# Masked chunk scores in three 256-column banks instead of two 512-column ones

## The chip, the cores and the metric

The kernel runs on one core of a Trainium2 chip. The metric is device time in microseconds (us): the median of three runs before is 471.69 us (471.17 to 472.49). A profile is one further execution; its times are read against its own span and its own device time, both given below.

## The reference

Two blocks follow each other. The first is a gated recurrence over four batches, eight heads, 768 steps and a head width of 48; the second is a feed-forward block on the 3072 resulting rows of 384.

```python
for t in range(S):                                   # attention, per batch and head
    state = alpha[t, :, None] * state + outer(k[t], v[t])
    y[t] = q[t] @ state
a = x @ w1; b = x @ w2                               # x: y with the heads side by side
out = ((a * b) @ w3) @ w_out                         # 384 -> 1024 -> 1024 -> 384
```

## The kernel before

The sequence is cut into 24 chunks of 128 steps (six per batch). In a chunk the recurrence becomes small matrix products: with k and q scaled by the running decays, the scores k q are masked to the causal triangle and multiplied with v, and a carried state T adds what came from earlier chunks. Eight heads are worked as four pairs: index j is the pair, i the head in it, and head i sits on partitions 64i to 64i+47.

The main loop (L689) has one turn per chunk. In turn n TensorE gets, in this order: `attend_state(n-1)` (L469, state times q), `scores(n)`, `transposed(n+1)` (L376), `attend(n-1)` (masked scores times v, L477 or L480), `outer(n)` (L388), and at the end `decays(n+3)` (L341). Between them stand pieces of the first matrix products of the feed-forward block, which keep TensorE busy: a piece is nine products of `exact` (L510) on two PSUM banks. From turn 10 on the number of pieces repeats as 3, 3, 2, 0; turns 9, 13, 17 and 21 have none. After the loop (`part1.close()`, L785) the feed-forward block alone goes on, and nearly all of it is L510.

All PSUM results come from one pool of eight banks of 128 partitions by 512 fp32 (`bank()`, L105). The framework that builds the program gives each request the bank that is freed first in its own plan of the program, and makes the first product into it wait for the reader that frees it. So which reader a product waits for depends on how many banks were asked for before it. The readers that matter here are: the mask on VectorE (L435) for scores; two copies on ScalarE (L378) for transposes; two copies on ScalarE (L484) for the attention result y; an exponential on ScalarE (L345) for the decays; an add on VectorE (L398) for the outer product; a scaled copy on ScalarE (L519) and an add on VectorE (L521) for the two banks of a gate piece. Instruction order on every engine is fixed when the program is built; the same plan decides, within limits written in the code (`issue_after`), how independent work such as the weight conversion (L238 to L260) is woven in.

Scores of chunks 0 to 7 are whole 128x128 squares (`scores`, L441). From chunk 8 (`TURNED`, the ninth) on, `turned_scores` (L417) leaves out the quarter that the mask would empty. With 64x64 blocks A (first half of the steps against the first), B (second against second) and C (k of the first half against q of the second), a matmul of 128 columns gives A and C of a head, one of 64 columns gives B. For head i=1 the halves of the partitions are swapped ("turned"), so that blocks of both heads can run in different quarters of the array at once: array rows by i, array columns by `part ^ i`. `attend_low` (L414) multiplies the A blocks of the chunk before with v between the score products; `attend` (L477) does B and C together. The masked scores lie in the tile `ms`, and `keep` and `keep_turned` hold the masks as integers for a bitwise and.

Of the kernel before, what the change touches and what calls it, by code (L numbers as in the profile page):

```python
# [12 lines left out]
I32 = mybir.dt.int32  # L13
# [3 lines left out]
ALU = mybir.AluOpType  # L17
# [31 lines left out]
def kernel(  # L49
# [12 lines left out]
    nc = tc.nc  # L62
    B, H, S, D = q.shape
    C = 128
    DM = H * D
    DF = moe_w1.shape[1]
    NCH = S // C
    N = B * NCH
    NP = H // 2
    DP = 64  # L70
# [13 lines left out]
    def pool(name, bufs, stack=ctx, **kw):  # L84
        return stack.enter_context(tc.tile_pool(name=name, bufs=bufs, **kw))
# [15 lines left out]
    p1 = pool("p1", 1, stack=part1, side="right", reuse_waits="tile")  # L101
# [3 lines left out]
    def bank():  # L105
        return ps.tile([C, 512], FP32, tag="bank", name="bank")

    st, mark = {}, {}
# [51 lines left out]
    def turned(n):  # L160
        return TURNED <= n < N
# [28 lines left out]
    sums = p1.tile([C, 2, C], FP32R, name="sums")  # L190
    signs = p1.tile([C, 2, C], FP32R, name="signs")
    keep = p1.tile([C, C], I32, name="keep")
    keep_turned = p1.tile([C, 2, DP], I32, name="keep_turned")
    qks = [p1.tile([C, 2, H, DP], FP32, name=f"qk{i}") for i in range(3)]
    Ts = [p1.tile([C, NP, DP], FP32, name=f"T{i}") for i in range(2)]
    decs = [p1.tile([C, 3, NP], FP32, name=f"dec{i}") for i in range(2)]
# [8 lines left out]
    nc.vector.tensor_scalar_mul(keep, utri, -1.0)  # L205
    keep_bc = keep[:, None, :].to_broadcast([C, NP, C])
    for half in range(2):
        nc.gpsimd.tensor_copy(out=keep_turned[ds(DP * half, DP), 1 - half], in_=keep[ds(DP * half, DP), ds(DP * half, DP)])
    nc.gpsimd.memset(keep_turned[DP:, 1], -1)
    for x in qks:  # L210
        nc.vector.memset(x[:, :, :, D:], 0.0)
    make_identity(nc, ident)
# [197 lines left out]
    def attend_low(n, jj, i, half):  # L410

        s, w = ds(DP * i, DP), (vts[n % 2] if i else st["v", n])
        h = half * NP // 2 + jj
        nc.tensor.matmul(st["y", n][0][i][ds(DP * half, DP), jj, 0:DP], w[s, h if i else 2 * h, :],  # L414
                         st["ms", n][s, i, h, 0:DP], start=(n % NCH == 0 and jj == 0), stop=True, skip_group_check=True)

    def turned_scores(n):  # L417

        qkT = st["qkT", n]
        sc = [bank().rearrange("p (j c) -> p j c", j=NP) for _ in range(2)]  # L420
        for j in range(NP):
            for part in range(2):
                for i in range(2):
                    r, t = ds(DP * i, D), slice(DP * part, C)
                    nc.tensor.matmul(sc[i][ds(DP * (part ^ i), DP), j, t], qkT[r, 0, j, ds(DP * part, DP)],  # L425
                                     qkT[r, 1, j, t], start=True, stop=True)
            if turned(n - 1):
                for i in range(2):
                    attend_low(n - 1, j % 2, i, i ^ (j < 2))
        ms = work.tile([C, 2, NP, C], FP32, tag="ms", name="ms")  # L430
        for i in range(2):
            r = ds(DP * i, DP)
            low, high = (keep_turned[r, 0], keep_turned[:, 1]) if i else (keep[r, 0:DP], keep[:, DP:])
            for x, mask, t in ((slice(DP * i, DP * (i + 1)), low, slice(0, DP)), (slice(0, C), high, slice(DP, C))):
                masked = nc.vector.tensor_tensor(ms[x, i, :, t].bitcast(I32), sc[i][x, :, t].bitcast(I32),  # L435
                                                 mask[:, None, :].to_broadcast([x.stop - x.start, NP, DP]),
                                                 op=ALU.bitwise_and)
        ends_of_part1[0] = mark["ms", n] = masked.ins
        st["ms", n] = ms

    def scores(n):  # L441
        if turned(n):
            return turned_scores(n)
        qkT = st["qkT", n]
        sc = [bank().rearrange("p (j c) -> p j c", j=NP) for _ in range(2)]
        for j in range(NP):
            for i in range(2):
                r = ds(DP * i, D)
                nc.tensor.matmul(sc[i][:, j, :], qkT[r, 0, j, :], qkT[r, 1, j, :], start=True, stop=True)  # L449
        ms = work.tile([C, 2, NP, C], FP32, tag="ms", name="ms")  # L450
        for i in range(2):
            masked = nc.vector.tensor_tensor(ms[:, i].bitcast(I32), sc[i].bitcast(I32), keep_bc, op=ALU.bitwise_and)
        ends_of_part1[0] = mark["ms", n] = masked.ins
        st["ms", n] = ms
# [17 lines left out]
    def attend(n):  # L472
        (y, heads), ms, vc = st.pop(("y", n)), st.pop(("ms", n)), st.pop(("v", n))
        for j, i, to in heads:
            if turned(n):
                w = vts[n % 2][:, j, :] if i else vc[:, 2 * j, :]
                nc.tensor.matmul(to[:, DP:], w, ms[:, i, j, DP:], start=False,  # L477
                                 stop=(j % HP == HP - 1), skip_group_check=True)
            else:
                nc.tensor.matmul(to, vc[:, 2 * j + i, :], ms[:, i, j, :], start=(n % NCH == 0 and j % HP == 0),  # L480
                                 stop=(j % HP == HP - 1), skip_group_check=True)
        x = work.tile([C, HP, 2, C], FP32, tag="x", name="x", bufs=4)
        for i in range(2):
            copied = nc.scalar.copy(x[:, :, i], y[i])  # L484
        ends_of_part1[1] = copied.ins
        x = x.rearrange("p j i t -> p (j i) t")

        g, c = divmod(n, G)
        to = xd[g].rearrange("(b h d) t -> b d h t", b=2, d=D)
        for half in range(2):  # L490
            later.append((to[half, :, :, ds(c * C, C)], x[ds(DP * half, D)]))
# [197 lines left out]
    for n in range(N + 1):  # L689
# [16 lines left out]
        if n < N:  # L706
            scores(n)
        else:
            for j in range(NP):
                for i in range(2):  # L710
                    attend_low(n - 1, j % 2, i, i ^ (j < 2))
# [34 lines left out]
        if n:  # L746
            attend(n - 1)
# [52 lines left out]
    low, high = range(FH), range(FH, KF)  # L800
# [74 lines left out]
```

## Time and profile before

| | |
|---|---|
| median of three runs | 471.69 us |
| profiled execution, device time | 472.93 us |
| its span on the core | 471.2 us |
| granted TensorE clock | 0.996 |
| TensorE (PE) busy | 453.1 us, 96% |
| VectorE (DVE) busy | 363.5 us, 77% |
| ScalarE (ACT) busy | 278.9 us, 59% |
| 64 mask operations L435 | 6.9 + 6.8 + 6.5 + 6.5 us |
| first turned score product | 69.5 us after the span's start |
| last turned score product | 178.5 us |

In the profile, a line of the group list names the source line, engine, operation, tile written and tile read, shapes and count, then busy time and mean duration, then idle time of that engine just before it and what ended the wait. PEld is TensorE's weight load. One fp32 matmul of the program is two passes, thus two PE instructions (a transpose is one); fp32r products are one. PE durations include the flow through the array and overlap, so a stretch's length is read from starts, not from sums of durations.

### The profile page before, as it was taken

What the parts mean: (1) busy time and instruction counts of PE and PEld (TensorE: products, weight loads), DVE (VectorE), ACT (ScalarE), POOL (GpSimd) and SP (SyncE); (2) the same over time, 40 slices, a digit from 0 to 9 for tenths busy, and PEclk for the clock granted to TensorE, in tenths of its full rate; (3) what the DMA queues carried; (4) which work ended last, traced back from release to release, by engine and by line L of the source; (5) the groups of instructions that cost most, each with busy time, mean ns of one, the idle gap of its engine ahead of it and who ended that gap; (6) DMA issues with size and microseconds to landing.
All of it is one profiled execution on the core that took longest, in us unless ns stands there. A gap on an engine that the chain in (4) does not pass through costs nothing.

```text
span 471.2 us, 11168 instructions
## 1 busy us (share of the span) xinstructions
PE 453.1 (96%) x4360; PEld 430.4 (91%) x4360; DVE 363.5 (77%) x610; ACT 278.9 (59%) x552; POOL 96.0 (20%) x186
## 2 busy tenths in 40 slices
PE   4996999999999999999999999999999999999996
PEld 2675889898999989999999999999999999999996
DVE  2876997999979898999999968764542977766771
ACT  4864975767767554889787656554553633333330
POOL 6332243234313550222221111111011000000000
PEclk9999999999999999999999999999999999999999
DMA  9999999999999953566685433212013886555511
GB/s 182 251 189 247 239 226 207 222 218 207 203 207 209 266 141 116 170 185 220 205 297 190 133 124 101 85 50 85 35 51 111 245 243 184 176 160 167 173 52 50
DMA packets 145668, 80.36 MB, mean 171 GB/s; under 512 B 96240, under 2 KB 137456, under 8 KB 145616
## 3 DMA queue, kind: packets, MB, share of 16 engines
q1 hardware_dynamic: 139840, 64.44, 55.2%
q0 software_dynamic: 5776, 15.22, 10.3%
q8 instruction: 34, 0.56, 0.5%
q14 instruction: 18, 0.15, 0.1%
HBM read 57.58 MB, written 22.06 MB: 169 GB/s over the span
## 4 chain that ended last, share of the span: by engine, by line
PE 86%; DMA 5%; DVE 4%; ACT 3%; issue 1%; SPq 0%; DVEq 0%; ACTq 0%
PE bank L510 70%; DMA kq<-in_q_dram 3%; PE bank L425 3%; PE bank L376 2%; PE bank L477 2%; PE bank L469 2%; PE bank L612 1%; PE bank L388 1%; PE bank L338 1%; PE bank L341 1%; DMA raw<-in_moe_w_dram 1%; PE bank L480 1%; DVE qk L354 1%; PE bank L414 1%; PE bank L449 1%
## 5 line engine op out<-in xcount | busy, mean ns | idle before, releaser
L510 PE MATMUL bank<-x,w 128*128 128x384 f32 x1152 | 212.4, 338 | 1.9 <-DVE ms L435 0.9
L510 PEld LDWEIGHTS bank<-x,w 128*128 128x128 f32 x1152 | 199.9, 188 | 4.4 <-DVE ms L435 1.0
L510 PE MATMUL bank<-w3o,ab 128*128 128x384 f32 x576 | 100.2, 336 | 0.0
L510 PEld LDWEIGHTS bank<-w3o,ab 128*128 128x128 f32 x576 | 99.8, 188 | 0.0
L535 ACT ACTIVATE bank<-bank 128x384 f32<-128x384 f32 x96 | 45.6, 476 | 43.0 <-PE bank L510 42.8
L519 ACT ACTIVATE t<-bank 128x384 f32<-128x384 f32 x64 | 31.6, 495 | 54.8 <-PE bank L510 54.6
L585 POOL DMA_DIRECT2D abd<-ab x45 | 25.7, 570 | 143.4 <-DVE ab L571 126.8
L571 DVE TENSOR_TENSOR ab<-bank,r 128x384 f32<-128x384 f32 x44 | 24.4, 555 | 25.6 <-ACT bank L535 16.4
L378 ACT COPY qkT<-bank 128x512 f32<-128x512 f32 x48 | 26.0, 591 | 24.2 <-PE bank L376 24.2
L641 DVE TENSOR_TENSOR ab<-abl,ab 128x1024 fp32r<-128x1024 f32 x24 | 29.4, 1224 | 13.0 <-ACT ab L640 13.0
L640 ACT ACTIVATE ab<-abl 128x1024 fp32r<-128x1024 f32 x24 | 25.5, 1061 | 20.2 <-PE bank L510 18.0
L510 PE MATMUL bank<-wo,w3T 128*128 128x384 f32 x192 | 35.9, 334 | 0.0
L354 DVE TENSOR_TENSOR qk<-kq,e 128x768 f32<-128x768 f32 x24 | 23.3, 971 | 15.0 <-ACT e L345 7.5
L510 PEld LDWEIGHTS bank<-wo,w3T 128*128 128x128 f32 x192 | 33.5, 188 | 0.0
L243 ACT ACTIVATE power<-power,rebias 128x512 uint32<-128x512 uint32 (+1 forms) x36 | 25.1, 700 | 12.2 <-DVE power L242 12.1
L521 DVE SCALAR_TENSOR_TENSOR o<-bank,t 128x384 f32<-128x384 f32 x24 | 13.4, 557 | 22.4 <-issue 13.7
L642 DVE SCALAR_TENSOR_TENSOR ab<-ab,abl 128x1024 fp32r<-128x1024 f32 x24 | 29.2, 1219 | 0.0
L521 DVE SCALAR_TENSOR_TENSOR r<-bank,t 128x384 f32<-128x384 f32 x40 | 22.1, 552 | 6.8 <-ACT t L519 4.1
L245 DVE SCALAR_TENSOR_TENSOR mant<-mant,rest 128x512 f32<-128x512 uint32 (+1 forms) x36 | 23.6, 655 | 2.0 <-ACT rest L238 1.9
L238 ACT ACTIVATE rest<-raw 128x512 f32<-128x512 uint32 (+1 forms) x36 | 23.4, 652 | 1.0 <-DMA raw<-in_moe_w_dram 1.0
L166 POOL COPY vt<-v 64x192 f32<-64x192 f32 x32 | 19.4, 606 | 22.0 <-DMA v<-in_v_dram 21.0
L246 DVE SCALAR_TENSOR_TENSOR power<-raw,power 128x512 uint32<-128x512 uint32 (+1 forms) x36 | 23.3, 655 | 0.3 <-ACT power L243 0.2
(104 smaller groups left out, 685.9 us busy)
## 6 DMA issues: line engine op xcount, KB each, us to landing
raw<-in_moe_w_dram SPq DMA_DIRECT2D x28, 512.0 KB, 5.3
abl<-abd SPq DMA_DIRECT2D x24, 512.0 KB, 4.3
abd<-ab POOLq DMA_DIRECT2D x45, 192.0 KB, 3.1
xT<-xd POOLq DMA_DIRECT2D x9, 576.0 KB, 4.4
kq<-in_k_dram SPq DMA_DIRECT2D x24, 192.0 KB, 5.0
kq<-in_q_dram SPq DMA_DIRECT2D x24, 192.0 KB, 5.8
xd<-x SPq DMA_DIRECT2D x48, 96.0 KB, 3.9
out_dram<-o SPq DMA_DIRECT2D x24, 192.0 KB, 3.4
```

What stands on the lines that cost most here:

```text
L243: nc.scalar.activation(power, power, AF.Relu, scale=2.0 ** 23, bias=rebias)
L354: mark["qk", n] = nc.vector.tensor_mul(qks[n % 3][:, :, :, 0:D], st.pop(("kq", n)), st.pop(("e", n)).rearrange("p i (h d) -> p i h d", h=H ...
L378: mark["qkT", n] = nc.scalar.copy(qkT[:, :, :, ds(DP * half, DP)], tp[half]).ins
L510: nc.tensor.matmul(p, w[part][i], x[part][i], start=start and part == parts[0] and i == 0, stop=stop and part == parts[-1] and i == n - 1, ...
L519: nc.scalar.activation(t, p1, AF.Copy, scale=(1.0 + 1.0 / P) * scale)
L521: nc.vector.scalar_tensor_tensor(to, p2, scale, t, op0=ALU.mult, op1=ALU.add)
L535: nc.scalar.activation(p, p, AF.Copy, scale=1.0 + 1.0 / P)
L571: nc.vector.tensor_mul(ab, p, r[0])
L585: (nc.gpsimd if late else nc.sync).dma_start(out=abd[g][:, f, :], in_=ab)
L640: nc.scalar.activation(t[:, 0], ab, AF.Copy, scale=1.0 - 2.0 ** -13)
L641: nc.vector.tensor_sub(t[:, 1], ab, t[:, 0].bitcast(FP32))
L642: nc.vector.scalar_tensor_tensor(t[:, 2], t[:, 0].bitcast(FP32), -1.0 - 1.0 / P, ab, op0=ALU.mult, op1=ALU.add)
```

## The change

The three kinds of blocks A, B and C get a bank each in place of one bank per head. Bank 0 takes the A blocks of both heads (head 0 on the lower partitions, head 1 on the upper), bank 1 takes B and C of head 0, bank 2 takes B and C of head 1; each bank uses 256 of its 512 columns. The 128-column matmul becomes two of 64 columns, so a chunk has 24 score matmuls in place of 16. `keep_turned` has a third plane, so that each bank is masked over all 128 partitions by one operation: three operations of 128x256 in place of four on 64x256 or 128x256 parts with strided rows. `attend_low` and `attend` read the new places in `ms`; their products are the same. The tile `ms` has the same size, and its last quarter stays unused. At the start, GpSimd makes the masks with four copies and two memsets in place of two and one.

```diff
-    keep_turned = p1.tile([C, 2, DP], I32, name="keep_turned")
+    keep_turned = p1.tile([C, 3, DP], I32, name="keep_turned")
...
     for half in range(2):
-        nc.gpsimd.tensor_copy(out=keep_turned[ds(DP * half, DP), 1 - half], in_=keep[ds(DP * half, DP), ds(DP * half, DP)])
-    nc.gpsimd.memset(keep_turned[DP:, 1], -1)
+        for x in (0, 2 - half):
+            nc.gpsimd.tensor_copy(out=keep_turned[ds(DP * half, DP), x], in_=keep[ds(DP * half, DP), ds(DP * half, DP)])
+        nc.gpsimd.memset(keep_turned[ds(DP * half, DP), 1 + half], -1)
...
         nc.tensor.matmul(st["y", n][0][i][ds(DP * half, DP), jj, 0:DP], w[s, h if i else 2 * h, :],
-                         st["ms", n][s, i, h, 0:DP], start=(n % NCH == 0 and jj == 0), stop=True, skip_group_check=True)
+                         st["ms", n][s, 0, h, :], start=(n % NCH == 0 and jj == 0), stop=True, skip_group_check=True)
...
-        sc = [bank().rearrange("p (j c) -> p j c", j=NP) for _ in range(2)]
+        sc = [bank()[:, 0:NP * DP].rearrange("p (j c) -> p j c", j=NP) for _ in range(3)]
         for j in range(NP):
-            for part in range(2):
+            for x, part, t in ((0, 0, 0), (1, 1, 1), (1, 0, 1)):
                 for i in range(2):
-                    r, t = ds(DP * i, D), slice(DP * part, C)
-                    nc.tensor.matmul(sc[i][ds(DP * (part ^ i), DP), j, t], qkT[r, 0, j, ds(DP * part, DP)],
-                                     qkT[r, 1, j, t], start=True, stop=True)
+                    r = ds(DP * i, D)
+                    nc.tensor.matmul(sc[x + x * i][ds(DP * (part ^ i), DP), j, :], qkT[r, 0, j, ds(DP * part, DP)],
+                                     qkT[r, 1, j, ds(DP * t, DP)], start=True, stop=True)
...
         ms = work.tile([C, 2, NP, C], FP32, tag="ms", name="ms")
-        for i in range(2):
-            r = ds(DP * i, DP)
-            low, high = (keep_turned[r, 0], keep_turned[:, 1]) if i else (keep[r, 0:DP], keep[:, DP:])
-            for x, mask, t in ((slice(DP * i, DP * (i + 1)), low, slice(0, DP)), (slice(0, C), high, slice(DP, C))):
-                masked = nc.vector.tensor_tensor(ms[x, i, :, t].bitcast(I32), sc[i][x, :, t].bitcast(I32),
-                                                 mask[:, None, :].to_broadcast([x.stop - x.start, NP, DP]),
-                                                 op=ALU.bitwise_and)
+        ms = ms.rearrange("p i j c -> p (i j c)")[:, 0:3 * NP * DP].rearrange("p (x j c) -> p x j c", x=3, j=NP)
+        for x in range(3):
+            masked = nc.vector.tensor_tensor(ms[:, x].bitcast(I32), sc[x].bitcast(I32),
+                                             keep_turned[:, x:x + 1, :].to_broadcast([C, NP, DP]), op=ALU.bitwise_and)
...
-                nc.tensor.matmul(to[:, DP:], w, ms[:, i, j, DP:], start=False,
+                nc.tensor.matmul(to[:, DP:], w, ms[:, 1 + i, j, :], start=False,
```

## The prediction

> **What bounds the kernel now.** I read the page's shares and slices, then busy times by stage, the group list, the waits of the stretch with turned scores, and the timeline around the longest waits.
>
> ```profile
> PE 453.1 (96%) x4360; PEld 430.4 (91%) x4360; DVE 363.5 (77%) x610; ACT 278.9 (59%) x552; POOL 96.0 (20%) x186
> PE   4996999999999999999999999999999999999996
> DVE  2876997999979898999999968764542977766771
> ```
>
> TensorE is full from the fourth slice on. VectorE is nearly as full until slice 23. By stage:
>
> ```profile
> 69.00:190.00 121.00, 118.86 (x2076) 109.88 (x2076) 108.79 (x212) 77.29 (x175) 38.13 (x69) 1.00 0.88 199
> 190.00:471.00 281.00, 277.54 (x1620) 276.93 (x1618) 203.60 (x310) 154.19 (x280) 32.21 (x53) 1.00 0.46 145
> ```
>
> After 190 us TensorE runs 277.5 of 281 us on work that the change does not touch: whatever part 1 loses or gains on TensorE moves the end by as much. From 69 to 190 VectorE is 90% busy (third figure), but only what makes TensorE wait counts. Its waits there:
>
> ```profile
> PE bank L510 <- DVE ms L435: 0.9, 2, 0.7
> PE bank L510 <- ACT qkT L378: 0.5, 1, 0.5
> PE bank L469 <- DVE ms L435: 0.3, 1, 0.3
> PE bank L425 <- ACT w L255: 0.2, 1, 0.2
> ```
>
> These are understated, since a matmul's modelled end covers the start of a gap. From the starts of single products, less the usual spacing, I get seven stalls, 2.85 us: 0.65 at 87.1 (bank freed by a copy L378), and 0.31 at 96.3, 0.37 at 110.9, 0.41 at 111.8, 0.14 at 140.1, 0.08 at 152.6, 0.89 at 173.8, whose bank a mask L435 frees: 2.2 us by masks. (The 0.2 put down to L255 is the 0.41 at 111.8: in the program that product waits for the fourth mask.)
>
> **What the Trainium skill says.** "TensorEngine Tiling (Array Packing)", Key Properties: tiles of the array work independently, and a change of tiling mode drains it. The trace agrees: score starts in each quarter keep their own rhythm, and 146 ns pass from the last 64-column start to the transposes, in place of about 60. "TensorE: Matmul & The Clock Gate", Part 3, says matmuls start strictly in program order; here they don't:
>
> ```profile
> 78.40 0.38 PE L425 MATMUL bank<-qkT 48*64 48x128 f32 x7
> 78.52 0.22 PE L414 MATMUL bank<-ms,v 64*64 64x64 f32 x1
> ...
> 78.53 0.27 PE L425 MATMUL bank<-qkT 48*64 48x128 f32 x1
> ```
>
> Eight score passes stand ahead of the first L414 in the program, and seven had started. The trace decides. "VectorE: DVE Perf Modes", Two Vector instructions with no wait between them: an operation whose operand starts in another group of 32 partitions than the last one's is held until earlier ones finish. The trace fits: mask 2 starts 0.33 us after mask 1 (both start at partition 0), mask 3 (partition 64) 0.44 after 2, mask 4 (0 again) 0.44 after 3. "PSUM — Partial Sum Buffer", Specifications, gives eight banks; the kernel's pool has all.
>
> **The change, part by part.**
>
> ```profile
> L425 PE MATMUL bank<-qkT 48*64 48x128 f32 x256 | 18.8, 271 | 0.2 <-ACT w L255 0.2
> L425 PE MATMUL bank<-qkT 48*64 48x64 f32 x256 | 16.0, 226 | 0.0
> L435 DVE TENSOR_TENSOR ms<-bank,keep_turned 64x256 int32<-64x256 int32 x16 | 6.9, 428 | 0.5
> L435 DVE TENSOR_TENSOR ms<-bank,keep_turned 128x256 int32<-128x256 int32 x16 | 6.8, 425 | 0.2
> L435 DVE TENSOR_TENSOR ms<-bank,keep 64x256 int32<-64x256 int32 x16 | 6.5, 407 | 0.0
> L435 DVE TENSOR_TENSOR ms<-bank,keep 128x256 int32<-128x256 int32 x16 | 6.5, 405 | 0.0
> ```
>
> *Score products.* In a quarter, 128-column passes start every 109 ns and 64-column ones every 58 (a run of nine in 524 ns). The two loaded quarters had 8 x 109 = 872 ns a chunk and get 16 x 58 = 928; the other two keep their 8 passes and run beside them. So the block grows by 0.05 us, to 1.27 from the measured 1.22. 16 x 0.052 = +0.83 us, all on the path. Bounds: half of 109 gives -0.2; 62 (what the transposes take) gives +2.0.
>
> *Masks.* Start to next start: 0.33 + 0.44 + 0.44 + 0.34 = 1.55 us a chunk. All three new ones start at partition 0, so should not be held: 3 x 0.33 = 1.0; held, 1.3. VectorE saves 16 x 0.55 = 8.8 us (at least 4). This is worth only what it takes off the 2.2 us.
>
> *Mask set-up* on GpSimd: three more operations of 0.15 to 0.23 us before 5 us; `sums`, which the first decay product needs, comes no later in the order built, so nothing. Memory traffic is the same.
>
> *The ninth bank request.* A turn without gate pieces asks for y 2, scores 2, transposes 2, outer 1, decays 1: eight, one round of the pool. With three score banks it is nine on eight, so each request reaches one release further. In the order built, on turns 10, 14, 18 and 22 the outer product (L388) or transposes wait for a reader that ran later, and so do the gate pieces behind:
>
> ```profile
> 84.74 0.62 PE L388 MATMUL bank<-v,qk 128*64 128x48 f32 x16
> 85.29 1.32 PE L510 MATMUL bank<-x,w 128*128 128x384 f32 x6
> 87.11 1.15 PE L510 MATMUL bank<-x,w 128*128 128x384 f32 x5 [0.49 <-ACT qkT L378]
> ```
> ```profile
> 84.70 0.52 ACT L345 ACTIVATE e<-bank 128x384 f32<-128x384 f32 x1
> 85.86 0.72 ACT L243 ACTIVATE power<-power,rebias 128x512 uint32<-128x512 uint32 x1 [0.64 <-DVE power L242]
> 86.49 1.05 ACT L378 COPY qkT<-bank 128x512 f32<-128x512 f32 x2
> ```
>
> Turn 10: today the outer product waits for an L484 long done, the first six gate products use the bank that L345 freed at 85.23, and the seventh waits for L378's first copy (87.07). Afterwards L388 waits for L345, and the *first* gate product for that L378. The six products that covered the wait now come after it: 6 x 0.19 = +1.16. ScalarE's copy is itself late because it stands behind L243.
>
> Turn 14: the stalls of 0.37 and 0.41 go, VectorE having saved six chunks; but TensorE then reaches L388 0.8 earlier and meets L345 (ends 113.82, was 0.4 ahead): 0.45 back, and 0.3 for a gate bank that the first mask frees: 0. Turn 18: -0.14; L345 ends 142.68, L388 would start at 142.37: +0.44; the tenth gate product waits for the first mask (145.2), +0.3: +0.6. At 151.4 a gate's first bank is now the first mask's (ready 152.12, and 0.14 to react): 0.9, less 0.3 for an earlier VectorE, less the 0.08: +0.5. Turn 22: -0.89; transposes wait for L484 (+0.4) and the tenth gate product for a mask (+0.7): +0.2. At 96.3 the stall goes: -0.31. Sum of waits: 1.16 + 0 + 0.6 + 0.5 + 0.2 - 0.3 = +2.15. What queues behind each wait on TensorE is all later work.
>
> *Order before chunk 8.* The new plan also reorders turns 5 and 6: ScalarE puts L243 ahead of both L484 copies, and L255 ahead of L319; VectorE puts L257 ahead of both L452 masks of chunk 6. L484 (50.55 and 52.43) ends at 53.05, so the transposes start 0.26 later; L319 moves behind a 0.6 us operation, which delays the decay product 0.16 more; and L271, in need of the bank that the first L452 frees, goes from 55.41 to 56.28 (L257 ends near 55.45, the mask 0.7 later). +0.87, with no gap on TensorE behind it until 85 to give it back.
>
> Sum: 0.83 + 2.15 + 0.87 = **+3.85 us**. The profiled execution's span becomes 475.1 (its own device time, 472.93, lies 1.7 above its span); on the median of 471.69 this gives **475.5 us**.
>
> **Rivals.**
>
> *VectorE relief pays.* All 2.2 us of mask stalls vanish and no longer reach is felt: 0.83 - 2.2 = -1.4, 470.3 us, so faster. For it: VectorE is 90% busy and frees six of seven stalled banks. It decides if L345 ends 0.6 us before L388 asks, on turn 10 (85.22 against 84.74) and after; the trace shows it 0.5 too late. With the early reordering it is 471.2, no change. Together 6%.
>
> *TensorE's own cost alone*: banks wait as long as before, +0.83, 472.5 us. It needs slack in the pool, and the turns without pieces have none. 10%.
>
> *The quarters don't run ahead.* If the three pairs of products per j go in lockstep, a j takes 3 x 2 x 58 = 348 ns where the loaded quarters need 232: 4 x 116 = 0.46 a chunk, 7.4 in all, 482.9 us. The timeline at 78.5 speaks against it. 5%.
>
> That the change doesn't do what it says is out: the built program has three masks and 24 products a chunk.
>
> **How the numbers follow.** Forecast 79%, rivals 6, 10 and 5. Low end: 58 becomes 54.5 (-0.2), all mask stalls go, ScalarE's stay (1.16 + 0.45 + 0.44 + 0.4 - 2.2 = 0.25), early +0.87: +0.9, 472.6. High end: 62 ns and held masks (+0.6): +5.7, 477.4. About 0.3% (1.4 us) is what a measurement here tells from no change; from the cases: slower 0.86, same 0.10, faster 0.04.
>
> **What would show it.** Score blocks 0.05 us longer and three masks 0.33 apart; L271 near 56.3; L388 on turn 10 waiting for L345 and then no gate product before L378's copy ends. Wrong if VectorE's saving shows as fewer stalls with none on ScalarE, if score blocks pass 1.4 us, or if TensorE's time after 190 us changes.

## The result, and the profile after

| | median | runs | ratio to before, 95% interval |
|---|---|---|---|
| before | 472.49 us (471.17 to 472.72) | 5 | |
| after | 475.69 us (474.61 to 476.46) | 5 | 1.0074 (1.0053 to 1.0095) |

The change costs 3.2 us. Ratios here and below compare mean times and leave out executions more than 1.5% above the fastest of the same kernel (five of the two masks with smaller stores, one of the kernel before). The profiled execution took 475.83 us with a span of 474.0 us; the one before had 472.93 and 471.2, so the two traces differ by 2.8 us. The shares and slices of the page after:

```profile
PE 456.3 (96%) x4616; PEld 432.8 (91%) x4616; DVE 356.6 (75%) x594; ACT 279.4 (59%) x552; POOL 95.6 (20%) x189
PE   4998999899999999999999999999999999999996
DVE  1896896989869687999999968855542877666761
```

VectorE lost 7 us of work (363.5 to 356.6) and TensorE gained 3. By stage (span of the stretch, then busy time and instructions of PE, PEld, DVE, ACT and POOL, then clock, DMA share and GB/s):

```profile
69.00:192.00 123.00, 118.88 (x2327) 110.47 (x2327) 101.21 (x193) 76.74 (x174) 36.66 (x69) 1.00 0.89 198
192.00:474.00 282.00, 278.36 (x1625) 277.77 (x1623) 204.32 (x312) 155.05 (x282) 32.55 (x53) 1.00 0.46 146
```

I matched the starts of TensorE's products in the two traces, in order. Where a distance after minus before is given below, it is from that. It is -0.14 us at 67 us, +2.82 at 184 us and unchanged from there to the end. So all of the loss comes from the stretch with turned scores. TensorE's waits there, as the list of waits has them (engine, line, releaser: total us, times, longest):

```profile
PE bank L508 <- DVE ms L434: 1.8, 4, 0.8
PE bank L508 <- ACT qkT L379: 1.0, 1, 1.0
PE bank L426 <- issue: 0.7, 1, 0.7
PE bank L415 <- POOL vt L166: 0.4, 1, 0.4
PE bank L389 <- ACT e L346: 0.2, 1, 0.2
```

(After the change L426 is the score product, L434 the mask, L377 the transpose, L379 its copy, L389 the outer product, L415 a product of the A blocks with v, L508 a gate product, L342 the decays, L346 their exponential.) Waits for a mask are 1.8 us in four places, where the same list before had 1.2 in three, although VectorE has less to do. Four things are new: gate products wait for the copy of the transposes at their start, score products stop for nothing that the trace names, products of A wait for a copy on GpSimd, and the outer product of turn 14 waits for the exponential, as the prediction had it there.

*The products and masks.* The groups by shape, and the three masks of chunk 9 on VectorE's timeline:

```profile
L426 PE MATMUL bank<-qkT 48*64 48x64 f32 x768 | 20.3, 221 | 0.7 <-issue 0.7
L434 DVE TENSOR_TENSOR ms<-bank,keep_turned 128x256 int32<-128x256 int32 x48 | 17.4, 413 | 0.3 <-PE bank L426 0.3
```
```profile
79.68 1.08 DVE L434 TENSOR_TENSOR ms<-bank,keep_turned 128x256 int32<-128x256 int32 x3
```

Three masks take 1.08 us; with 0.41 for the last one they start 0.33 apart. The block of score products of chunk 9 goes from its first product to the first transpose. Before it began at 78.40, as the prediction shows; this is its end on TensorE's timeline of before, then both lines of after:

```profile
79.61 0.40 PE L376 MATMUL bank<-ident,qk 64*128 64x64 f32 x6
```
```profile
78.31 0.33 PE L426 MATMUL bank<-qkT 48*64 48x64 f32 x9
...
79.59 0.40 PE L377 MATMUL bank<-ident,qk 64*128 64x64 f32 x6
```

1.28 us in place of 1.22. Wherever nothing else stops the block, it is 0.054 to 0.057 longer: 0.9 us for 16.

*Turn 10.* TensorE's timeline after, then ScalarE's:

```profile
83.69 0.21 PE L426 MATMUL bank<-qkT 48*64 48x64 f32 x1 [0.73 <-issue]
...
85.75 0.62 PE L389 MATMUL bank<-v,qk 128*64 128x48 f32 x16
87.38 3.39 PE L508 MATMUL bank<-x,w 128*128 128x384 f32 x18 [1.01 <-ACT qkT L379]
90.61 0.51 PE L342 MATMUL bank<-la,sums 128*128 128x384 f32 x2
```
```profile
86.14 0.72 ACT L244 ACTIVATE power<-power,rebias 128x512 uint32<-128x512 uint32 x1 [0.97 <-DVE power L243]
86.76 1.05 ACT L379 COPY qkT<-bank 128x512 f32<-128x512 f32 x2
```

Before, six gate products ran from 85.29 and the seventh at 87.11, once its bank was copied. Now none runs until the first copy of the two is out (half of 1.05 us after 86.76), and all 18 come behind it. The decays L342 begin at 90.61, against 89.32 before.

### The profile page after: what moved, and what is told of

The parts are those of the page before. It is cut to its first block, busy times and chain, and to the rows that moved or that the text cites. A ratio compares the mean times of both kernels' runs of the same rounds, so it can differ in the third digit from the quotient of the medians.

```text
span 474.0 us, 11644 instructions
## 1 busy us (share of the span) xinstructions
PE 456.3 (96%) x4616; PEld 432.8 (91%) x4616; DVE 356.6 (75%) x594; ACT 279.4 (59%) x552; POOL 95.6 (20%) x189
## 4 chain that ended last, share of the span: by engine, by line
PE 83%; DVE 8%; ACT 3%; issue 3%; DMA 2%; SPq 0%; DVEq 0%; ACTq 0%
PE bank L508 70%; PE bank L426 2%; PE bank L377 2%; PE bank L467 2%; PE bank L610 1%; DMA kq<-in_q_dram 1%; DVE x L502 1%; PE bank L475 1%; PE bank L336 1%; DVE qk L355 1%; ACT x L500 1%; DVE ms L450 1%; ACT qkT L379 1%; PE bank L342 1%; PE bank L389 1%
## 5 line engine op out<-in xcount | busy, mean ns | idle before, releaser
L508 PE MATMUL bank<-x,w 128*128 128x384 f32 x1152 | 211.8, 338 | 3.0 <-DVE ms L434 1.8
L508 PEld LDWEIGHTS bank<-x,w 128*128 128x128 f32 x1152 | 200.0, 188 | 5.0 <-DVE ms L434 2.7
L508 PE MATMUL bank<-w3o,ab 128*128 128x384 f32 x576 | 100.2, 336 | 0.0
L508 PEld LDWEIGHTS bank<-w3o,ab 128*128 128x128 f32 x576 | 99.9, 188 | 0.0
L379 ACT COPY qkT<-bank 128x512 f32<-128x512 f32 x48 | 26.1, 596 | 26.4 <-PE bank L377 26.4
L508 PE MATMUL bank<-wo,w3T 128*128 128x384 f32 x192 | 35.9, 334 | 0.0
L508 PEld LDWEIGHTS bank<-wo,w3T 128*128 128x128 f32 x192 | 33.5, 188 | 0.0
L501 DVE TENSOR_TENSOR x<-xT,x 128x1152 fp32r<-128x1152 f32 x14 | 19.0, 1356 | 4.8 <-ACT x L500 4.7
```

The source lines that it names most:

```text
L379: mark["qkT", n] = nc.scalar.copy(qkT[:, :, :, ds(DP * half, DP)], tp[half]).ins
L508: nc.tensor.matmul(p, w[part][i], x[part][i], start=start and part == parts[0] and i == 0, stop=stop and part == parts[-1] and i == n - 1, ...
```

## The experiments

Each experiment was timed beside the kernel before on the same chip. In the four groups of experiments the kernel before had medians of 472.41 us (27 executions: early order, cut products, two masks, third bank), 472.63 (43: eight requests, four masks, and the kernel before and the cut products with smaller stores), 472.55 (28: the whole change, the two masks and the bare request with smaller stores) and 472.60 (27: third bank with smaller stores).

**The mask set-up and the early order alone.** The kernel before with the third plane of `keep_turned`, made by the four copies and two memsets of the change; the masks read the same values from other places. The build of it moves the same early instructions as the change does.

```diff
-    keep_turned = p1.tile([C, 2, DP], I32, name="keep_turned")
+    keep_turned = p1.tile([C, 3, DP], I32, name="keep_turned")
...
-            low, high = (keep_turned[r, 0], keep_turned[:, 1]) if i else ...
+            low, high = (keep_turned[r, 0], keep_turned[:, 2]) if i else ...
```

> The kernel before with nothing but the mask set-up of the change: three planes, made by four copies and two memsets; scores and the four masks as before. In the order built it carries the same swap on turns 5 and 6 as the change (L243 ahead of both L484, L255 ahead of L319, L257 ahead of both L452). Forecast's theory: the swap costs 0.87 us on TensorE, so +0.9 us (ratio 1.002), L271 0.9 us later against its neighbours. Rival: the part before chunk 8 is paced by loads and by VectorE, which give it back before 57 us: 0 us, and TensorE reaches the first gate product (about 58.3 us) no later than before.

Measured: 472.49 us (22 executions), ratio 1.0005 (0.9988 to 1.0021). No cost of the early order shows. The interval reaches to +1.0 us and so doesn't exclude 0.87 by itself; the traces do. TensorE is 0.6 us ahead of the kernel before at 67 us here, and the product of the weight conversion that the prediction put at 56.28, with VectorE's L257 ahead of it, came no more than 0.2 us late (the kernel before, this one, the kernel after):

```profile
55.41 0.69 PE L271 MATMUL bank<-w,signs 128*128 128x512 f32 x1
...
55.33 0.69 PE L272 MATMUL bank<-w,signs 128*128 128x512 f32 x1
...
55.60 0.50 PE L272 MATMUL bank<-w,signs 128*128 128x512 f32 x1
```

**Products cut in two, nothing else.** Two banks and four masks as before, 24 products of 64 columns.

```diff
-            for part in range(2):
+            for part, half in ((0, 0), (1, 1), (0, 1)):
...
-                    r, t = ds(DP * i, D), slice(DP * part, C)
+                    r, t = ds(DP * i, D), ds(DP * half, DP)
```

> The kernel before with only the products cut: each 128-column score product becomes two of 64 columns into the same two banks; four masks as before. 24 products a chunk. Theory: each score block 0.055 us longer, 16 blocks, +0.9 us (ratio 1.002), no wait moved to another reader. Rival, TensorE's own cost is the bulk of the change's +3.2 us, by more instructions to fetch and issue: +2.5 us or more, with gaps inside score blocks that no semaphore ends.

Measured: 476.82 us (6 executions), ratio 1.0086 (1.0063 to 1.0109). The blocks are 0.057 us longer, as expected, but that is 0.9 us of 4.4: in size the rival's value came, though the gap isn't in a score block. TensorE stops for 3.3 us in the middle of an outer product whose instructions wait for no semaphore, and from 115.8 us on the granted clock is 0.50 for 6.8 us (second fence: a stretch as above, which ends just after that; its mean clock, 0.54, stands after the five engines):

```profile
113.01 0.27 PE L388 MATMUL bank<-v,qk 128*64 128x48 f32 x2
116.37 0.99 PE L388 MATMUL bank<-v,qk 128*64 128x48 f32 x14 [3.10 <-issue]
```
```profile
118.00:123.00 5.00, 5.00 (x18) 5.00 (x18) 1.25 (x2) 0.98 (x2) 1.99 (x4) 0.54 0.83 152
```

The packets of the trace point to what stops it: a transfer of 16 KB on the instruction queue runs from 113.97 to 114.90, and TensorE goes on 1.48 us after its end. Every stop of this kind ends so. In the 14 traces of this case there are 14 stops of 0.35 us or more (from one start of a weight load to the next) between 60 and 192 us that no semaphore explains and that fall inside a run of like instructions; all end 1.28 to 1.61 us after such a transfer. In the kernel after, the transfer ended at 82.19 and the score products went on at 83.69. The six kernels with 24 products a chunk have ten of the stops, 13.1 us together, or 2.2 each; the other eight have four, 2.8 us together. In the whole execution the queue has 36 transfers in the kernel after and 34 in the kernel before:

```profile
q8 instruction: 36, 0.59, 0.6%
```
```profile
q8 instruction: 34, 0.56, 0.5%
```

That the transfers carry TensorE's instructions is worked out, not shown: 34 of 16 KB are 64 bytes for each of its 8,720 products and weight loads, and 36 the same for 9,232. And that the stops wait for the transfers rests on this agreement in time; no run changed these transfers alone.

**Two masks, two banks.** Full 128-column products throughout; the quarter that the mask empties is computed, too, and each bank is masked by one 128x512 operation, for which `keep_turned` becomes a whole 128x128 mask.

```diff
-                    r, t = ds(DP * i, D), slice(DP * part, C)
+                    r, t = ds(DP * i, D), slice(0, C)
...
+            mask = keep_turned if i else keep
+            masked = nc.vector.tensor_tensor(ms[:, i].bitcast(I32), sc[i].bitcast(I32),
+                                             mask[:, None, :].to_broadcast([C, NP, C]), op=ALU.bitwise_and)
```

> Two banks per chunk as before, but the 64-column product is widened to 128 columns too (the quarter that the mask empties is computed and masked away), so that each bank is masked by one operation of 128x512: two masks, no third bank, 16 products. Theory: the score block stays at 1.22 us, because the quarters that get more were idle; two masks take 2 x 0.60 = 1.2 us in place of 1.55, free the banks after 0.68 and 1.28 us in place of 0.79 and 1.68, and with no ninth request no wait moves to ScalarE: about half of the 2.2 us of mask stalls goes, -1 us (ratio 0.998). Rival, VectorE's time is worth nothing here: 0 us. Rival, the quarters are not independent: block 1.5 us or more, +4 us.

Measured: 477.92 us (6 executions), ratio 1.0117 (1.0097 to 1.0138). None of the three expected values came. The block stays at 1.22 us with a third more score columns in it, so the quarters of the array do run independently, and the two that had spare time fill it. The time goes in one place. TensorE's and GpSimd's waits between 107 and 118 us:

```profile
PE bank L413 <- POOL vt L166: 3.9, 1, 3.9
POOL dec L404 <- DMA dec<-ends: 5.1, 1, 5.1
```

GpSimd waits for a small transfer of its own and does the copy that TensorE needs only after that; the clock is 0.50 for 6.8 us from 113.2 us on, while TensorE still waits. So this run doesn't tell what VectorE's time is worth.

**A third bank request alone.** The kernel before with one more bank per chunk, an 8-column product into it and a small copy out of it (result unused).

```diff
+        extra = bank()[0:DP, 0:8]
+        nc.tensor.matmul(extra, qkT[0:D, 0, 0, 0:DP], qkT[0:D, 1, 0, 0:8], start=True, stop=True)
...
+        nc.vector.tensor_copy(out=work.tile([DP, 8], FP32, tag="extra", name="extra"), in_=extra)
```

> The kernel before with a third bank asked for in each turned chunk: one extra product of 8 columns into it (its result is not used) and one VectorE copy of 64x8 ahead of the masks, which frees it. Two score banks, 16 + 1 products, four masks. Theory, the ninth request is what costs: waits as in the change without VectorE's relief, so +2.5 to +3.5 us (ratio 1.005 to 1.007), on turn 10 no gate product before the copy L378 ends, 1.2 us later than before. Rival, the request is harmless and only the work counts: 16 x 0.1 us on TensorE's path at most, +0.3 to +1.0 us, and the first gate product on turn 10 starts when the outer product ends.

Measured: 476.32 us (6 executions), ratio 1.0073 (1.0046 to 1.01). Turn 10, TensorE's timeline:

```profile
87.28 0.67 PE L388 MATMUL bank<-v,qk 128*64 128x48 f32 x16 [0.24 <-ACT e L345]
89.14 4.09 PE L513 MATMUL bank<-x,w 128*128 128x384 f32 x13 [1.19 <-ACT qkT L378]
```

This is what the prediction foresaw for the change: the outer product waits for L345, and the first gate product waits for the copy L378. The request with its small product does it, with 16 score products and four masks as before. The time, at the top of the expected range, is not clean: in this trace the clock is halved for 3.4 us after this wait and for 6.8 us at 52 us, and the extra product costs 0.087 us per block, 1.4 us for 16.

**Eight requests again.** The kernel after, with the outer product written into free columns of the first score bank of its chunk.

```diff
-        s1 = bank()[:, 0:NP * D].rearrange("p (j d) -> p j d", j=NP)
+        s1 = (st.pop(("free", n)) if turned(n) else bank())[:, 0:NP * D].rearrange("p (j d) -> p j d", j=NP)
...
-        sc = [bank()[:, 0:NP * DP].rearrange("p (j c) -> p j c", j=NP) for _ in range(3)]
+        banks = [bank() for _ in range(3)]
+        st["free", n] = banks[0][:, NP * DP:]
+        sc = [x[:, 0:NP * DP].rearrange("p (j c) -> p j c", j=NP) for x in banks]
```

> The changed kernel (24 products of 64 columns and three masks a chunk), but the outer product L389 writes into columns 256 to 447 of the first score bank of its own chunk instead of asking for a bank, so that a turn without gate pieces asks for eight banks again. Theory (the ninth request costs what the moved waits cost, about 2.1 us): the first gate product of turn 10 no longer waits 1.0 us for the copy that frees its bank, and the time comes to 0 to +0.9 us over the kernel before, 472.4 to 473.4, which is 2 us or more below the changed kernel's 475.7. Rival 1 (the cost lies in the products and whatever they do to other work, not in the banks): it stays at 475 to 477. Rival 2 (transfers set the pace up to 120 us, and whoever runs ahead of them stalls for 4 us and runs on a halved clock, as the two kernels with a split product or two masks did near 113 us): 476 to 478, with a stall of over 3 us between 105 and 120 us.

Measured: 479.01 us (6 executions), ratio 1.013 (1.0106 to 1.0154): none of the three. The edit brought a wait of its own, because the outer product now has to wait for the mask that reads its bank, of the same chunk. Its line in the list of waits between 60 and 192 us, and turn 10 on the timeline:

```profile
PE bank L389 <- DVE ms L436: 4.3, 6, 1.3
```
```profile
85.81 1.32 PE L510 MATMUL bank<-x,w 128*128 128x384 f32 x6
87.30 0.61 PE L510 MATMUL bank<-x,w 128*128 128x384 f32 x2 [0.18 <-ACT qkT L379]
```

As a price of the request it failed. For turn 10 it is telling all the same: with eight requests, three masks and 24 products, six gate products run ahead of the copy again, as in the kernel before.

**VectorE's saving taken back.** The kernel after with its first mask as two operations of 64 partitions.

> The changed kernel with its first mask cut into two operations of half the partitions, so that VectorE does four operations a chunk again and each bank comes free 0.1 to 0.4 us later. If VectorE's saving is worth something in the changed kernel (the waits for a mask, 1.8 us in all, grow with it), 0.5 to 2 us above the changed kernel: 476.2 to 477.7. If it is worth nothing, 475.2 to 476.2.

Measured: 477.53 us (6 executions), ratio 1.01 (1.0078 to 1.0123), so 1.2 to 1.8 us above the kernel after, as expected if the saving counts. It does not follow that the saving is worth that: waits for a mask at the gate products are 1.8 us here as there, and the trace is 2.1 us longer from 62 us on with two stops without a semaphore (1.8 us at 82 us, 1.3 at 116) where the kernel after had one of 1.0, and a half-clock window at 84 us. The worth of the saving stays open in the changed kernel.

**The same with fewer bytes to move.** The stops at 110 to 118 us come behind a stretch in which the DMA engines are busy all the time: in the cut products their share is 1.04 from 108 to 113 us. (In the stop itself, from 114 to 116, it falls to 0.13, so the engines weren't full to its end.) So I cut the stores of the first two groups' gate results from 384 columns to 8. Their issues and waits stay; the rest of these results isn't stored, and the last stage reads the third group's in their place, so these kernels serve for timing only. I ran the kernel before and its parts with that.

```diff
+            w = 8 if g < 2 and not late else TG
-            (nc.gpsimd if late else nc.sync).dma_start(out=abd[g][:, f, :], in_=ab)
+            (nc.gpsimd if late else nc.sync).dma_start(out=abd[g][:, f, 0:w], in_=ab[:, 0:w])
...
-            nc.sync.dma_start(out=st["abl", n], in_=abd[g][:, :, ds(c * C, C)])
+            nc.sync.dma_start(out=st["abl", n], in_=abd[max(g, 2)][:, :, ds(c * C, C)])
```

> The kernel before, with the stores of the first two groups' gate results cut from 384 columns to 8 (the rest of these results is not stored, and the last stage reads the third group's in their place): about 190 KB less per store, some 20 stores between 75 and 140 us, all issues and waits kept. It is the measure for the next kernel. If the kernel before is seldom held by transfers: 470.5 to 472.5. If transfers set its pace: below 470.

> The kernel with nothing but the products cut in two (measured at 476.8, with a stall of 3.3 us at 113 us and a halved clock after it), with the same smaller stores as the kernel before in this call (the rest of the first two groups' gate results is not stored). If the stall is transfers that come late in a stretch where all queues are full, it goes, and the kernel is 0.9 us above the lightened kernel before (at most 1.5). If the stall belongs to the products themselves (more instructions to be fetched, or the order of the work), it stays, and the kernel is 3 to 5 us above it.

> The changed kernel with the smaller stores of the lightened kernels (of the first two groups' gate results only 8 of 384 columns are stored, and the last stage reads the third group's in their place). The lightened kernel before came to 472.1. Theory (products +0.9, ninth request about +2.1, neither having to do with transfers): 3 us above that, 474.6 to 475.8. If the changed kernel's loss comes from transfers that land late: 1.5 us or less above it, up to 473.6.

> The kernel before with a third score bank asked for and used by one 8-column product and one 64x8 copy (result unused), with the smaller stores of the lightened kernels. The extra product lengthens each of the 16 score blocks by 0.087 us, as measured with full stores: 1.4 us. Theory (the ninth request itself costs about 2.1 us, transfers or not): 3.5 us above the lightened kernel before (472.1), 474.9 to 476.2. If the request costs nothing and the kernel with full stores lost the rest by late transfers and a halved clock: 473.2 to 473.8.

> The kernel with two whole-bank masks, two score banks and 128-column products throughout (it computes the empty quarter and masks it), with the same smaller stores. With full stores it took 477.9, 5.5 us more than the kernel before, and stalled 3.9 us at 110 us on a tile of v that had not come, with a halved clock after it. If that is transfers: the stall goes, VectorE's saving takes up to 2.2 us of mask waits, and it is at or below the lightened kernel before, 470 to 472.5. If it is the order of the work: it stays 4 us or more above, 476 or more.

| smaller stores, and | median, executions | ratio to before, 95% interval | full stores |
|---|---|---|---|
| nothing else | 472.11 us, 22 | 0.9984 (0.9969 to 0.9999) | 1 |
| products cut in two | 473.99 us, 22 | 1.003 (1.0012 to 1.0048) | 1.0086 |
| third bank request and product | 474.37 us, 22 | 1.0038 (1.0022 to 1.0055) | 1.0073 |
| the whole change | 474.73 us, 7 | 1.0051 (1.0027 to 1.0075) | 1.0074 |
| two masks, two banks | 477.93 us, 22 | 1.0076 (1.0051 to 1.01) | 1.0117 |

The kernel before hardly cares for the bytes. The cut products do: of their 4.4 us about 2 are left, between the two values expected. The stop of 3.3 us shrank to 0.9, in the same place (the product before it starts at 113.62):

```profile
114.55 0.61 PE L388 MATMUL bank<-v,qk 128*64 128x48 f32 x14 [0.66 <-issue]
```

The change as a whole keeps its loss, 0.0067 of 472.6 or 3.2 us over the lightened kernel before, as expected if transfers that land late are not its cause. The parts come to 2.2 us (cut products) and 2.5 us (third request), of which 1.4 are the extra product's: 2.2 + 1.1 = 3.3 us. That matches the whole with nothing left for VectorE's saving, but each figure is good to about 1 us, so a saving of that size is not excluded. Both values expected for the third request were missed, from either side. In its trace the wait on turn 10 is 1.78 us, and the clock is 0.50 for 3.4 us from 86.2 us on, just before its end; TensorE had come there 1.2 us earlier than in the lightened kernel before, and lost that first.

The two masks did not settle. The profiled execution took 471.71 us without any long stall, and in it nothing was gained or lost on balance after 62 us (distance to the lightened kernel before: -0.88 there, -0.84 at the end). But 16 of the 22 executions took 476.9 to 479.3 us, and none of these was profiled. Fewer bytes from these stores do not cure them; what does is open.

**The request without a product.** The lightened kernel before with a third bank that VectorE sets to zero in 64x8 elements after the chunk's last mask.

> The lightened kernel before with one more bank request per chunk from the ninth on and nothing on TensorE for it: the bank is set to zero in 64x8 elements by VectorE right after the chunk's last mask (about 0.1 us of VectorE a chunk), and its content isn't used. It prices the ninth request alone. Theory: +1.5 to +3 us over the lightened kernel before, 473.6 to 475.1, with a wait of the first gate product on turn 10 for the copy L378 of about 1.2 us. If requests cost nothing, and the loss of the changed kernel and of the kernel with a third bank lies in their products: 472 to 472.6.

Measured: 480.98 us (6 executions), ratio 1.0193 (1.0163 to 1.0224), a miss for both. The build put the outer product ahead of `attend` on TensorE, and the gate products then wait 4.6 us for masks, in four places. It changed the order as well as the request and prices neither. So the request was never timed quite alone.

No variant that does all the work was faster than the kernel before; with the smaller stores the kernel before was by 0.16%, just beyond the interval.

## Why the prediction was right, and where it was not

The time was right (475.5 predicted, 475.69 measured), and so was the direction. Of the steps of its sum, two held in the traces, one fell, and the base was low. That the last two cancel is luck.

- *Score products, +0.052 us a block.* 0.057 in the traces, 0.9 us for 16; the prediction's own 928 less 872 ns gives 0.056, so 0.052 was a slip. (Likewise its lower bound, half of 109 ns, gives no change and not -0.2.) As a length of the block it is right. As the cost of 24 products it is too small: cut products alone cost 2.2 us with smaller stores. The missing term is the stops without a semaphore, and the sum had none. In the profiled execution of the kernel after that stop (1.0 us at 83 us) is nearly all hidden, because the wait for ScalarE on turn 10 stands right behind it; ScalarE's copy starts 0.27 us later than before, so by this working about that much of it remains.
- *Masks, 3 x 0.33 us.* Measured 0.33 apart. What the Trainium skill says in "VectorE: DVE Perf Modes", Two Vector instructions with no wait between them, holds: with every operand starting at partition 0, none is held.
- *The ninth request, +2.15 us.* The distances between the traces, place by place, less 0.057 for a block:

| place | predicted | measured |
|---|---|---|
| turn 10 | +1.16 | +1.26 |
| 96.3 us | -0.31 | -0.35 |
| turn 14 | 0 | -0.01 |
| turn 18 | +0.6 | +0.85 |
| 151.4 us | +0.5 | +0.26 |
| turn 22 | +0.2 | +0.12 |
| sum | +2.15 | +2.13 |

 Turn 10 came as worked out, up to one detail: the outer product did not wait for the decays' exponential, as TensorE had been held up 1.0 us before it. On turn 14 it did (0.4 us from the starts), a gate product behind it waited for the first mask, and the two old stalls went, all as foreseen. Turn 22 is right in part by chance: the stall of 0.89 at the tenth gate product went, and 0.9 came for a mask at the seventh (0.7 at the tenth was foreseen); but the transposes didn't wait for L484, a stop of 0.4 without a semaphore at 169.8 went, and 0.6 came from a wait for GpSimd's copy that nobody foresaw. By the times, with smaller stores, the request is worth about 1.1 us and not 2.1; how the loss divides between request and cut products is known to about 1 us.
- *Order before chunk 8, +0.87 us: wrong.* The kernel with the set-up alone shows no difference, and the change is 0.14 us ahead at 67 us. The failed step is "with no gap on TensorE behind it until 85 to give it back". TensorE alone doesn't set this stretch: in the kernel after it was 1.9 us ahead at 42.5 us and level again at 56. On the way it did wait 0.5 us for the copy on ScalarE that the new order puts behind L243 (L482 in that kernel), but it had come there early, and the wait took only its lead.
- *The base.* The median of three runs, 471.69, lay 0.8 us under what 27 to 43 runs of the same kernel give. The predicted rise of 3.85 us was 0.65 too much, and the base too low by nearly as much.

The rivals: that VectorE's relief makes the kernel faster is refuted by the time, and 1.8 us of waits for masks remain in four places; what the relief is worth by itself stays open. TensorE's own cost alone (+0.83) is refuted by the cut products, at 4.4 us with full stores and 2.2 with smaller ones, and by turn 10. Quarters in lockstep is refuted by a block of 1.28 us, and by the two-mask kernel, whose block did not grow though it computes the empty quarter, too.

## What to carry to other kernels

When tiles come from a pool with as many requests per turn as buffers, one request more shifts every wait behind it by a reader; write down, for the products behind it, which reader each now waits for and when that reader runs, since work that covered the wait may now stand behind it. Splitting matmuls costs instructions too: where the DMA engines are busy throughout, look at the stops without a semaphore and count how many of TensorE's instructions the stage gains. And take the base from many runs where the forecast is below 1%.

## What the runs showed of the hardware

- *TensorE can stop without a semaphore, most likely for its instructions.* There were 14 stops of 0.35 to 3.4 us, and all ended 1.28 to 1.61 us after a 16 KB transfer on the instruction queue. I had looked at waits with a releaser only; in TensorE's waits of the kernel before one line was a sign of it:

```profile
PE bank L376 <- issue: 0.2, 1, 0.2
```

- *A stop has a second price.* In five traces the granted clock was 0.50 for 3.4 or 6.8 us between 84 and 123 us, each time towards the end of a pause of 1.4 to 4.2 us between product starts or up to 0.4 us after it (below: the third bank request with full stores; the stretches before and after it have 1.00). The Trainium skill, "TensorE: Matmul & The Clock Gate", Part 1: The HAM clock gate, has half rate after an idle window of about 3.4 us. The lengths agree with such windows, but a pause of 1.4 us was enough once, and pauses of up to 1.9 us were not in other traces.

```profile
89.50:92.90 3.40, 3.40 (x13) 3.40 (x12) 3.21 (x10) 2.05 (x6) 0.97 (x2) 0.50 0.93 201
```

- *Being early can cost.* The cut products and the two masks came to 110 us 1.1 to 1.4 us ahead of the kernel before and left 123 us 4.6 to 5.0 us behind it, with the same 24.2 to 24.5 MB moved by 110 us in all three. It looks as if a lead over the transfers was taken back, with half a clock on top; no run shows it apart from the rest, and the profiled two masks with smaller stores kept their lead.
